# Five column blocks for six in the first MLP layer, and a shorter activation, in a windowed-attention and two-MLP kernel

## The chip, the cores and the metric

The kernel runs on one core of one Trainium2 chip. The metric is the device time of one execution in microseconds; times before are from three runs on the chip, and one further execution was profiled.

## The reference

Inputs are q, k, v of 4 batches, 8 heads, 576 positions and 64 dimensions in float32, and two pairs of weights in float64: w_in (512 x 2048) and w_out (2048 x 512), one pair for each MLP.

```
scores = (1/8) q @ k^T
heads 0-3: keep 0 <= i-j < 32;  heads 4-7: keep 0 <= i-j < 128 and (i-j) % 4 == 0
attn = softmax(scores) @ v                     # then laid out as x: 2304 tokens x 512
h = x @ w_in;  x = (h * 1/(1+exp(-1.702 h))) @ w_out      # first MLP
h = x @ w_in2; out = (max(h, 0)^2) @ w_out2               # second MLP
```

## The kernel before, in words

**Layout.** Activations lie transposed: the 512 features are four groups of 128 partitions, the tokens are columns. In the first layer the 2304 columns are cut in six blocks (`BLOCKS1`) of 512, 256, 384, 512, 256 and 384 columns. A block is a list of pieces (batch, residue of the position modulo 4, from, to), so a block's columns come from one or two batches. The second layer has five blocks (`BLOCKS2`): 512, 256, 512, 512, 512.

**A step.** For each block sixteen steps (`step`) run over the 2048 hidden features, 128 at a time. Operands are split in a high part that the matmul's float32r format holds and a remainder, and each product is three matmuls: high x high, high x low and low x high. A step is 12 matmuls into a hidden tile h (lines 587 to 589), the activation on ScalarE and VectorE (lines 609 to 645), its rounding gh and remainder gl, and 12 matmuls from them into four output banks o (lines 673 to 675), which collect over all sixteen steps. h has two PSUM banks, o four, s (scores, transposes and values of attention) two. At a block's last step the o banks are evacuated to ost tiles (two places) and stored to x2d in DRAM; the second layer loads them from there and splits them.

**The activation of the first layer** is formed as min(exp(1.702 h), 1) x h x (1 + |tanh(0.851 h)|), twice the wanted value; the evacuation scales by 0.5. It takes tanh and the exponential on ScalarE, the absolute value on ScalarE or VectorE, and two products on VectorE (lines 626 and 629). The second layer has a relu and a square.

**Weights.** Each layer has 32 weight tiles, two a step. One is loaded as float64 bits (`raw`, three places), the top half word of each number is copied to a tile c by a cast (line 309, by the helper at line 236 or 238; c has three places), joined with the rest by VectorE (line 312), and split in wh and wl. The first layer's tiles are prepared while block 0 runs and stay for all blocks; the second layer's take their places in the last block of the first layer, each when its last reader is done.

**Attention.** A batch is eight units (a pair of heads and half of the positions). A unit loads qk and v, makes 12 scores matmuls (line 451), masked maxima on VectorE (467), exponentials on ScalarE (474), a normalisation (242 or 244), a transpose (on TensorE at line 524 and a copy for batches 0 and 1, 32 x 32 bands on VectorE into a cleared tile pt for batches 2 and 3, line 509), 12 value matmuls (543), and copies of the result, high and remainder, to the x tile of the block that owns the columns (555 and 559). Batch 0 runs ahead of the first layer, batch 1 in block 0, batch 2 in block 2 and batch 3 in block 3. The x tiles have three places x0, x1, x2 for blocks n, by n modulo 3, of 512, 256 and 384 columns.

**Order.** No order is written out. `Schedule` is a planner: each task has estimated costs on the engines that may do it, predecessors, buffers and a due time (want). It takes, again and again, the task that can start first by its own clock, ties by the due time, and so fixes each engine's instruction order; which of ScalarE and VectorE does a copy is its choice too, with penalties against VectorE (`SPARE_ACT`). Due times of block steps follow from `begin`, which adds up matmul times and an allowance for attention (`T_ATT`); those of attention units are spread over the block that holds their batch. The estimates affect the order only.

Of the kernel before, what the change touches and what calls it, by code (L numbers as in the profile page):

```python
# [35 lines left out]
UQ, UK, UV = HALF, HALF + PAD, NBLK * P  # L36

T_START = 26.0
T_ATT = 12.0
A0 = 0.0  # L40
A1 = 1.0
DEFER = 0.0
BAND_FROM = 2
W2_GAP = 4.0
WARM = 256
MASK_AT = -9.0
LEAD = (12.0, 8.0, 5.0)
SPACE = 4.0
C_BUFS = 3
RAW_BUFS = 3  # L50
IDLE = (0.3, 0.3)
SPARE_POOL = (3.0, 3.0, 0.0)
# [1 line left out]
SPARE_TO = (15.0, 160.0)  # L54


_HALF_BLOCKS = [
# [3 lines left out]
]  # L61
BLOCKS1 = [[(b + g, r, a, e) for b, r, a, e in blk] for g in (0, 2) for blk in _HALF_BLOCKS]
BLOCKS2 = [512, 256, 512, 512, 512]


class Schedule:
# [18 lines left out]
    def buffer(self, cls):  # L85
        return {"cls": cls, "held": False, "left": 0, "end": 0.0}

    def task(self, engine, cost, want, fn, after=(), bufs=(), port=False):


        many = isinstance(engine, tuple)
        t = {
            "ways": dict(zip(engine, cost)) if many else {engine: cost}, "many": many,
            "want": want, "fn": fn, "bufs": bufs, "port": port,
            "left": 0, "ready": [], "next": [], "n": len(self.tasks), "end": None,
        }
        for a in after:
            a["next"].append(t)
            t["left"] += 1
        for b in bufs:  # L100
            b["left"] += 1
        self.tasks.append(t)
        return t
# [83 lines left out]
def attention_mlp_mlp(  # L187
# [33 lines left out]

    places = {
        "o": 4, "h": 2, "s": 2, "raw": RAW_BUFS, "c": C_BUFS, "qk": 2, "v": 3, "sm": 2, "st": 3, "pt": 1,
        "x0": 1, "x1": 1, "x2": 1, "xx": 1, "raw2": 3, "g": 2, "e": 1, "gh": 2, "gl": 2, "ost": 2,
    }
    for f in range(KF):
        for part in range(2):
# [37 lines left out]
    def dve1(n):  # L265
        return 0.062 + n / 960
# [20 lines left out]
    def weights(layer, f, part, want):  # L287


        m = {}  # L290
        raw_b, c_b, w_b = buffer("raw"), buffer("c"), buffer(f"w{f}_{part}")
        name = f"{f}_{part}"

        def load():

            m["raw"] = wst.tile([P, DM, 2], U32, tag="raw", bufs=RAW_BUFS, name="raw")
            nc.sync.dma_start(
                m["raw"].rearrange("p n t -> p (n t)").bitcast(U16)[:, 0:4 * DM - 1],
                (w1, w2)[layer][f, part].bitcast(U16)[:, 1:4 * DM],
            )  # L300

        def top(e):

            m["c"] = tops[top_count[0] % C_BUFS]
            top_count[0] += 1
            halves = m["raw"].rearrange("p n t -> p (n t)").bitcast(BF16).rearrange("p (n t) -> p n t", t=4)[:, :, 2]
            copy(e, m["c"].bitcast(F16).rearrange("p (n t) -> p n t", t=2)[:, :, 1], halves)

        def join():
            V.scalar_tensor_tensor(
                out=m["raw"][:, :, 0], in0=m["raw"][:, :, 0], scalar=13, in1=m["c"],
                op0=ALU.logical_shift_right, op1=ALU.bitwise_or,
            )

        def value():
            return m["raw"][:, :, 0].bitcast(F32)

        def high_part(e):  # L320
            wh[layer, f, part] = wpool.tile([P, DM], F32R, tag="wh" + name, name="wh" + name)
            copy(e, wh[layer, f, part], value())

        def low_part(e):
            wl[layer, f, part] = wpool.tile([P, DM], F32R, tag="wl" + name, name="wl" + name)
            minus(e, wl[layer, f, part], value(), wh[layer, f, part])

        t = task("dma", 1.456, want - LEAD[0], load, (), [raw_b])
        t = task(("act", "dve"), (0.57, 0.602), want - LEAD[1], top, [t] + tops_zero, [raw_b, c_b], True)
        t = task("dve", 0.602, want - LEAD[1], join, [t], [raw_b, c_b], True)  # L330
        hi = task(*copies(DM), want - LEAD[2], high_part, [t], [raw_b, w_b], True)
        lo = task(*pairs(DM), want - LEAD[2], low_part, [hi], [raw_b, w_b], True)
        split_task[layer, f, part] = [hi, lo]
        wbuf[layer, f, part] = w_b


    x_t, x_buf, x_done = {}, {}, {}
    x_first = {}

    def x_tile(n):  # L340
        if n not in x_t:
            size = 512 if n % 3 == 0 else sum(e - a for _, _, a, e in BLOCKS1[n])
            x_t[n] = xpool.tile([P, 2, KD, size], F32R, tag=f"x{n % 3}", name=f"x{n % 3}")
        return x_t[n]

    def x_pieces(b, p, u):
# [57 lines left out]
    def attend(b, p, u, want, start, turn_pe, i):  # L404
# [144 lines left out]
        att_tasks.append(pv)  # L549
        for n, w, src_, dst_ in x_pieces(b, p, u):  # L550
            if n not in x_buf:
                x_buf[n] = buffer(f"x{n % 3}")

            def to_hi(e, n=n, src_=src_, dst_=dst_):
                copy(e, dst_(x_tile(n), 0), src_(m["o"]))

            def to_lo(n=n, src_=src_, dst_=dst_):
                x = x_tile(n)
                V.tensor_tensor(out=dst_(x, 1), in0=src_(m["o"]), in1=dst_(x, 0), op=ALU.subtract)  # L559

            t = task(("act", "dve"), (0.07 + w / 1340, dve1(w)), want, to_hi, [pv], [pv_b, x_buf[n]])
            t2 = task("dve", dve1(w), want, to_lo, [t], [pv_b, x_buf[n]])
            x_done.setdefault((n, p), []).extend([t, t2])
# [5 lines left out]
    def step(layer, blk, f, want, a=0, z=None):  # L569
# [29 lines left out]
        def g():  # L599
            if "g" not in m:  # L600
                m["g"] = gpool.tile([P, 512], F32, tag="g", name="g")[:, 0:n]
            return m["g"]

        def h():
            return m["h"][:, 0:n]

        if layer == 0:

            e_b = buffer("e")

            def tanh():
                A.activation(out=g(), in_=h(), func=AF.Tanh, scale=0.851)  # L612

            def exp():
                m["e"] = gpool.tile([P, 512], F32, tag="e", bufs=1, name="e")[:, 0:n]
                A.activation(out=m["e"], in_=h(), func=AF.Exp, scale=1.702)

            def absolute(e):
                if e == "act":
                    A.activation(out=g(), in_=g(), func=AF.Abs)  # L620
                else:
                    gb = g().bitcast(U32)
                    V.tensor_scalar(out=gb, in0=gb, scalar1=0x7FFFFFFF, scalar2=None, op0=ALU.bitwise_and)

            def times_h():
                V.scalar_tensor_tensor(out=g(), in0=g(), scalar=1.0, in1=h(), op0=ALU.add, op1=ALU.mult)  # L626

            def times_e():
                V.scalar_tensor_tensor(out=g(), in0=m["e"], scalar=1.0, in1=g(), op0=ALU.min, op1=ALU.mult)  # L629

            a1 = task("act", 0.145 + n / 1536, want, tanh, [t], [h_b, g_b])
            a2 = task("act", 0.145 + n / 1536, want, exp, [t], [h_b, e_b])
            a1 = task(*copies(n), want, absolute, [a1], [g_b], True)
            a1 = task("dve", dve1(n), want, times_h, [a1], [g_b, h_b])
            last = task("dve", dve1(n), want, times_e, [a1, a2], [g_b, e_b], True)
        else:

            def relu():
                A.activation(out=g(), in_=h(), func=AF.Relu)  # L639

            def square(e):
                by_name[e].tensor_tensor(out=g(), in0=g(), in1=g(), op=ALU.mult)  # L642

            t = task("act", 0.145 + n / 1536, want, relu, [t], [h_b, g_b])
            last = task(*pairs(n), want, square, [t], [g_b], True)
# [96 lines left out]

    begin = []
    now = T_START
    att_blocks = (0, 2, 3)
    for n, size in enumerate(sizes1):
        begin.append(now)
        now += KF * 24 * mm(size) + (T_ATT if n in att_blocks else 0)
    begin2 = []
    for size in BLOCKS2:  # L750
        begin2.append(now)
# [4 lines left out]
        attend(0, p, u, T_START - (nu - i) * SPACE, True, True, i)  # L756
    if WARM:
        task("pe", 0.0, T_START, warm_end, list(att_tasks), [warm_b])
    for b in range(1, B):
        if b == BAND_FROM:  # L760
            zero_task = task(
                "pool", 0.7, begin[att_blocks[b - 1]] - 5, lambda: G.memset(pt, 0.0), list(att_tasks), [buffer("pt")]
            )
        blk = att_blocks[b - 1]
        span = begin[blk + 1] - begin[blk]
        for i, (p, u) in enumerate(ORDER):
            late = span * DEFER if b % 2 and i >= nu - 2 else 0.0
            attend(b, p, u, begin[blk] + span * (A0 + A1 * i / nu) + late, False, b < BAND_FROM, b * nu + i)

    def order(layer):  # L770
        ks = [(f, 0) for f in range(2)]
# [34 lines left out]
    for n, size in enumerate(BLOCKS2):  # L806
        c0 = sum(BLOCKS2[:n])
        want = begin2[n]
        cls = ("xx", "x1", "x0", "xx", "x0")[n]
        blk = {"i": n, "n": size, "c0": c0, "buf": buffer(cls), "done": {}}  # L810
        blk["x"] = lambda blk=blk: blk["tile"]
        blk["ready"] = lambda k, blk=blk: blk["done"][k]
# [122 lines left out]
```

## Time and profile before

| what | value |
|---|---|
| runs | 902.05, 902.67, 903.28 us (median 902.67) |
| profiled execution | 902.65 us |
| span of its instructions | 900.5 us |
| mean granted clock | 0.997 of 2.4 GHz |
| ScalarE, VectorE busy | 447.5, 506.0 us |
| HBM read, written | 54.73, 9.44 MB |

The span runs from the first to the last instruction of the core; the execution's time has 2.15 us around it. Busy times are sums over the whole span, over stages that differ, so a share of the span says little about one stage. A matmul's recorded duration overlaps its neighbours': what a stream of them costs is read from start to start.

### The profile page before, as it was taken

What the parts mean: (1) busy time and instruction counts of PE and PEld (TensorE: products, weight loads), DVE (VectorE), ACT (ScalarE), POOL (GpSimd) and SP (SyncE); (2) the same over time, 40 slices, a digit from 0 to 9 for tenths busy, and PEclk for the clock granted to TensorE, in tenths of its full rate; (3) what the DMA queues carried; (4) which work ended last, traced back from release to release, by engine and by line L of the source; (5) the groups of instructions that cost most, each with busy time, mean ns of one, the idle gap of its engine ahead of it and who ended that gap; (6) DMA issues with size and microseconds to landing.
All of it is one profiled execution on the core that took longest, in us unless ns stands there. A gap on an engine that the chain in (4) does not pass through costs nothing.

```text
span 900.5 us, 13900 instructions
## 1 busy us (share of the span) xinstructions
PE 884.7 (98%) x5145; PEld 758.4 (84%) x5145; DVE 506.0 (56%) x1427; ACT 447.5 (50%) x1211; POOL 2.6 (0%) x10
## 2 busy tenths in 40 slices
PE   7899999999999999999999999999999999999998
PEld 5677778999998777899999788899888888888887
DVE  6888887646788777755989722242322332222223
ACT  7999998545557555543666622232322222222222
POOL 0000000000000000000000000000000000000000
PEclk9999999999999999999999999999999999999999
DMA  6555563101122110110755500020000010000001
GB/s 227 187 156 195 194 208 133 32 12 44 47 58 83 34 44 16 54 60 1 247 194 194 189 1 0 1 94 1 24 1 0 13 48 1 1 23 24 1 1 47
DMA packets 28115, 65.06 MB, mean 72 GB/s; under 512 B 3120, under 2 KB 10800, under 8 KB 28048
## 3 DMA queue, kind: packets, MB, share of 16 engines
q1 hardware_dynamic: 28048, 64.18, 21.8%
q8 instruction: 40, 0.66, 0.3%
q14 instruction: 27, 0.22, 0.1%
HBM read 54.73 MB, written 9.44 MB: 71 GB/s over the span
## 4 chain that ended last, share of the span: by engine, by line
PE 74%; ACT 11%; DVE 7%; DMA 6%; issue 2%; SPq 0%; DVEq 0%; ACTq 0%
PE h L587 12%; PE o L673 12%; PE h L588 12%; PE h L589 12%; PE o L675 12%; PE o L674 12%; DMA raw<-in_w 5%; ACT sm L474 2%; ACT c L236 2%; ACT sm L242 2%; PE s L451 2%; DVE wl L247 1%; PE pv L543 1%; DVE g L626 1%; DVE g L629 1%
## 5 line engine op out<-in xcount | busy, mean ns | idle before, releaser
L673 PE MATMUL o<-gh,wh 128*128 128x512 f32 (+2 forms) x704 | 248.6, 353 | 1.9 <-ACT ost L242 1.2
L675 PE MATMUL o<-gl,wh 128*128 128x512 f32 (+2 forms) x704 | 247.6, 352 | 0.4 <-DVE gl L247 0.3
L674 PE MATMUL o<-gh,wl 128*128 128x512 f32 (+2 forms) x704 | 246.4, 350 | 0.0
L587 PE MATMUL h<-x,wh 128*128 128x512 f32 (+2 forms) x580 | 203.2, 350 | 1.2 <-DVE g L626 1.0
L589 PE MATMUL h<-x,wl 128*128 128x512 f32 (+2 forms) x580 | 198.8, 343 | 0.5 <-DVE wl L247 0.5
L588 PE MATMUL h<-x,wh 128*128 128x512 f32 (+2 forms) x580 | 198.6, 342 | 0.0
L642 DVE TENSOR_TENSOR g<-g 128x512 f32<-128x512 f32 (+1 forms) x81 | 51.2, 632 | 205.3 <-ACT g L639 204.6
L639 ACT ACTIVATE g<-h 128x512 f32<-128x512 f32 (+1 forms) x81 | 44.5, 550 | 219.0 <-PE h L589 218.0
L673 PEld LDWEIGHTS o<-gh,wh 128*128 128x128 f32 x704 | 132.9, 189 | 20.1 <-ACT gh L236 1.9
L675 PEld LDWEIGHTS o<-gl,wh 128*128 128x128 f32 x704 | 132.8, 189 | 18.8 <-DVE gl L247 3.2
L236 ACT CAST gh<-g 128x512 fp32r<-128x512 f32 (+2 forms) x166 | 90.2, 543 | 112.9 <-DVE g L629 55.7
L674 PEld LDWEIGHTS o<-gh,wl 128*128 128x128 f32 x704 | 132.9, 189 | 14.7
L247 DVE TENSOR_TENSOR gl<-g,gh 128x512 fp32r<-128x512 f32 (+2 forms) x177 | 104.4, 590 | 67.2 <-ACT gh L236 64.1
L587 PEld LDWEIGHTS h<-x,wh 128*128 128x128 f32 x580 | 110.3, 190 | 15.5 <-DVE g L626 1.7
L589 PEld LDWEIGHTS h<-x,wl 128*128 128x128 f32 x580 | 110.0, 190 | 11.0 <-DVE wl L247 0.8
L588 PEld LDWEIGHTS h<-x,wh 128*128 128x128 f32 x580 | 110.2, 190 | 9.9 <-DVE x L559 0.8
L474 ACT ACTIVATE sm<-sm,st 96x128 f32<-96x128 f32 x180 | 70.6, 395 | 12.7 <-DVE st L467 12.7
L612 ACT ACTIVATE g<-h 128x512 f32<-128x512 f32 (+2 forms) x96 | 46.8, 488 | 52.1 <-PE h L589 50.7
L626 DVE SCALAR_TENSOR_TENSOR g<-g,h 128x512 f32<-128x512 f32 (+2 forms) x96 | 52.7, 550 | 16.9 <-ACT g L620 13.0
L629 DVE SCALAR_TENSOR_TENSOR g<-e,g 128x512 f32<-128x512 f32 (+2 forms) x96 | 53.1, 553 | 1.2
L589 PE MATMUL h<-xx,wl 128*128 128x512 f32 x128 | 49.8, 389 | 0.0
L588 PE MATMUL h<-xx,wh 128*128 128x512 f32 x128 | 49.8, 389 | 0.0
(70 smaller groups left out, 831.0 us busy)
## 6 DMA issues: line engine op xcount, KB each, us to landing
raw<-in_w SPq DMA_DIRECT2D x64, 511.8 KB, 4.0
qk<-in_qkv SPq DMA_DIRECT2D x32, 304.0 KB, 2.9
v<-in_qkv SPq DMA_DIRECT2D x32, 192.0 KB, 2.9
raw<-x2d SPq DMA_DIRECT2D x16, 256.0 KB, 2.9
out_T<-ost SPq DMA_DIRECT2D x14, 256.0 KB, 2.1
x2d<-ost SPq DMA_DIRECT2D x8, 256.0 KB, 2.3
x2d<-ost SPq DMA_DIRECT2D x8, 192.0 KB, 2.0
x2d<-ost SPq DMA_DIRECT2D x8, 128.0 KB, 2.6
```

What stands on the lines that cost most here:

```text
L236: A.copy(out, in_)
L247: by_name[e].tensor_tensor(out=out, in0=a, in1=b, op=ALU.subtract)
L474: A.activation(out=m["sm", j][:, i], in_=m["sm", j][:, i], func=AF.Exp, bias=m["st"][:, 0, j, i:i + 1], scale=-1.0, accum_out=m["st"][:, 1 ...
L587: T.matmul(out, w_hi[:, ks], x[:, 0, k, a:z], start=(k == 0), stop=False)
L588: T.matmul(out, w_hi[:, ks], x[:, 1, k, a:z], start=False, stop=False)
L589: T.matmul(out, w_lo[:, ks], x[:, 0, k, a:z], start=False, stop=(k == KD - 1))
L626: V.scalar_tensor_tensor(out=g(), in0=g(), scalar=1.0, in1=h(), op0=ALU.add, op1=ALU.mult)
L629: V.scalar_tensor_tensor(out=g(), in0=m["e"], scalar=1.0, in1=g(), op0=ALU.min, op1=ALU.mult)
L642: by_name[e].tensor_tensor(out=g(), in0=g(), in1=g(), op=ALU.mult)
L673: T.matmul(out, w_hi[:, ds_], m["gh"], start=(f == 0 or extra), stop=False)
L674: T.matmul(out, w_lo[:, ds_], m["gh"], start=False, stop=False)
L675: T.matmul(out, w_hi[:, ds_], m["gl"], start=False, stop=(f == KF - 1))
```

## The change

The first layer has five blocks of 512, 512, 256, 512 and 512 columns; the second layer's blocks become 512, 512, 256, 512, 512. Places of x are assigned by a list: blocks 0 and 3 have x0 (512), 1 and 4 have x2 (512), 2 has x1 (256). Batch 1's eight units stay in block 0, batch 2's go to block 1, six of batch 3's to block 2 and two to block 3 (`UNITS`); the allowance is 2.4 us a unit in place of 12 us a batch. The activation is h x (1 + tanh(0.851 h)), with no exponential, absolute value or second product, and the tile e is gone. The c tiles are two for three. The estimate of the cast to c becomes 0.67 us on ScalarE and 0.38 us on VectorE, from 0.57 and 0.602. `DEFER`, which was 0, is gone, and pt is cleared with a due time of 8 us ahead of batch 2's first unit, from 5 us ahead of its block.

```diff
-T_ATT = 12.0
+T_ATT = 2.4
-C_BUFS = 3
+C_BUFS = 2
-_HALF_BLOCKS = [
+BLOCKS1 = [
     [(0, 0, 0, 144), (0, 1, 0, 144), (0, 2, 0, 144), (0, 3, 0, 80)],
-    [(0, 3, 80, 144), (1, 0, 0, 144), (1, 1, 0, 48)],
-    [(1, 1, 48, 144), (1, 2, 0, 144), (1, 3, 0, 144)],
+    [(0, 3, 80, 144), (1, 0, 0, 144), (1, 1, 0, 144), (1, 2, 0, 144), (1, 3, 0, 16)],
+    [(1, 3, 16, 144), (2, 0, 0, 128)],
+    [(2, 0, 128, 144), (2, 1, 0, 144), (2, 2, 0, 144), (2, 3, 0, 144), (3, 0, 0, 64)],
+    [(3, 0, 64, 144), (3, 1, 0, 144), (3, 2, 0, 144), (3, 3, 0, 144)],
 ]
-BLOCKS1 = [[(b + g, r, a, e) for b, r, a, e in blk] for g in (0, 2) for blk in _HALF_BLOCKS]
-BLOCKS2 = [512, 256, 512, 512, 512]
+UNITS = (8, 8, 6, 2)
+BLOCKS2 = [512, 512, 256, 512, 512]
...
-        t = task(("act", "dve"), (0.57, 0.602), want - LEAD[1], top, [t] + tops_zero, [raw_b, c_b], True)
+        t = task(("act", "dve"), (0.67, 0.38), want - LEAD[1], top, [t] + tops_zero, [raw_b, c_b], True)
...
+    x_place = ("x0", "x2", "x1", "x0", "x2")
...
-            e_b = buffer("e")
             def tanh():
                 A.activation(out=g(), in_=h(), func=AF.Tanh, scale=0.851)
-            def exp():
...
-            def absolute(e):
...
             def times_h():
                 V.scalar_tensor_tensor(out=g(), in0=g(), scalar=1.0, in1=h(), op0=ALU.add, op1=ALU.mult)
-            def times_e():
-                V.scalar_tensor_tensor(out=g(), in0=m["e"], scalar=1.0, in1=g(), op0=ALU.min, op1=ALU.mult)
             a1 = task("act", 0.145 + n / 1536, want, tanh, [t], [h_b, g_b])
-            a2 = task("act", 0.145 + n / 1536, want, exp, [t], [h_b, e_b])
-            a1 = task(*copies(n), want, absolute, [a1], [g_b], True)
-            a1 = task("dve", dve1(n), want, times_h, [a1], [g_b, h_b])
-            last = task("dve", dve1(n), want, times_e, [a1, a2], [g_b, e_b], True)
+            last = task("dve", dve1(n), want, times_h, [a1], [g_b, h_b])
...
-    att_blocks = (0, 2, 3)
-        now += KF * 24 * mm(size) + (T_ATT if n in att_blocks else 0)
+        now += KF * 24 * mm(size) + (T_ATT * UNITS[n] if n < len(UNITS) else 0)
...
+    wants = []
+    for n, count in enumerate(UNITS):
+        span = begin[n + 1] - begin[n]
+        wants += [begin[n] + span * A1 * (A0 + i) / count for i in range(count)]
...
-            attend(b, p, u, begin[blk] + span * (A0 + A1 * i / nu) + late, False, b < BAND_FROM, b * nu + i)
+            attend(b, p, u, wants[(b - 1) * nu + i], False, b < BAND_FROM, b * nu + i)
...
-        cls = ("xx", "x1", "x0", "xx", "x0")[n]
+        cls = ("xx", "x0", "x1", "x2", "xx")[n]
```

## Rows read from the trace of the kernel before

**Rows 1.** The page: engine, busy us (share of the span), instructions.

```profile
PE 884.7 (98%) x5145; PEld 758.4 (84%) x5145; DVE 506.0 (56%) x1427; ACT 447.5 (50%) x1211; POOL 2.6 (0%) x10
```

**Rows 2.** Four stretches: length, busy (instructions) by engine, granted clock, DMA share, GB/s.

```profile
19.00:47.00 28.00, 24.68 (x218) 17.14 (x215) 25.57 (x139) 27.95 (x122) 0.00 (x0) 1.00 0.55 175
47.00:147.00 100.00, 98.98 (x570) 77.91 (x570) 83.82 (x222) 96.08 (x266) 0.58 (x1) 0.98 0.57 188
...
275.40:378.20 102.80, 102.80 (x587) 81.33 (x586) 79.70 (x283) 59.61 (x188) 0.00 (x0) 1.00 0.15 46
...
427.90:500.90 73.00, 72.06 (x399) 67.63 (x398) 65.39 (x130) 50.21 (x100) 0.00 (x0) 1.00 0.66 215
```

**Rows 3.** TensorE in order of time, two second-layer blocks: start us, duration us, what.

```profile
639.72 0.39 PE L589 MATMUL h<-x,wl 128*128 128x512 f32 x1
...
644.93 0.39 PE L674 MATMUL o<-gh,wl 128*128 128x512 f32 x1
...
599.79 0.28 PE L675 MATMUL o<-gl,wh 128*128 128x256 f32 x1
...
602.91 0.28 PE L588 MATMUL h<-x,wh 128*128 128x256 f32 x1
```

**Rows 4.** Groups by line, TensorE, 47 to 147 us: count | busy us, mean ns.

```profile
L543 PE MATMUL pv<-pt,v 128*64 128x96 f32 x96 | 6.5, 256 | 0.5 <-ACT pt L236 0.5
L451 PE MATMUL s<-qk 64*96 64x128 f32 x84 | 6.3, 282 | 0.0
L524 PE MATMUL tp<-ident,sm 96*128 96x96 f32 x42 | 5.6, 253 | 0.0
```

**Rows 5.** Groups by line, TensorE, 275.4 to 378.2 us.

```profile
L451 PE MATMUL s<-qk 64*96 64x128 f32 x86 | 6.8, 282 | 0.0
L543 PE MATMUL pv<-pt,v 128*64 128x96 f32 x108 | 6.4, 254 | 0.0
```

**Rows 6.** Chain that ended last, attention in blocks 2 and 3: start us, us, what.

```profile
213.33 0.83 PE s L451 x12
...
274.60 0.83 PE s L451 x12
...
348.08 0.65 PE pv L543 x12
...
360.90 0.65 PE pv L543 x12
```

**Rows 7.** Waits, 47 to 147 us: who for whom, us in total, times, longest.

```profile
DVE raw L312 <- ACT c L236: 4.2, 11, 0.6
...
PE h L587 <- DVE g L626: 1.0, 1, 1.0
```

**Rows 8.** One stretch, columns as in rows 2.

```profile
49.40:52.80 3.40, 3.40 (x10) 2.62 (x9) 3.27 (x8) 3.29 (x10) 0.00 (x0) 0.50 0.50 182
```

**Rows 9.** Waits, 427.9 to 510 us.

```profile
PEld o L675 <- DVE gl L247: 2.6, 8, 0.6
PEld o L673 <- ACT gh L236: 1.9, 4, 0.6
...
PE o L673 <- ACT ost L242: 1.2, 1, 1.2
```

**Rows 10.** Groups by line and shape, whole span: count | busy us, mean ns | idle before.

```profile
L236 ACT CAST c<-raw 128x512 f16<-128x512 bf16 x53 | 40.3, 782 | 10.9 <-DMA raw<-in_w 10.7
...
L629 DVE SCALAR_TENSOR_TENSOR g<-e,g 128x512 f32<-128x512 f32 x32 | 21.9, 684 | 0.1
...
L616 ACT ACTIVATE e<-h 128x512 f32<-128x512 f32 x32 | 19.0, 595 | 0.1
...
L629 DVE SCALAR_TENSOR_TENSOR g<-e,g 128x384 f32<-128x384 f32 x32 | 17.7, 552 | 0.2
...
L620 ACT ACTIVATE g<-g 128x512 f32<-128x512 f32 x16 | 10.2, 637 | 0.0
...
L238 DVE CAST c<-raw 128x512 f16<-128x512 bf16 x11 | 5.1, 462 | 3.9 <-DMA raw<-in_w 3.8
```

More of the change, by code (lines that the diff above doesn't have):

```diff
@@ L38 @@
 T_START = 26.0
-T_ATT = 12.0
+T_ATT = 2.4
 A0 = 0.0
 A1 = 1.0
-DEFER = 0.0
 BAND_FROM = 2
@@ L223, in attention_mlp_mlp @@
         "o": 4, "h": 2, "s": 2, "raw": RAW_BUFS, "c": C_BUFS, "qk": 2, "v": 3, "sm": 2, "st": 3, "pt": 1,
-        "x0": 1, "x1": 1, "x2": 1, "xx": 1, "raw2": 3, "g": 2, "e": 1, "gh": 2, "gl": 2, "ost": 2,
+        "x0": 1, "x1": 1, "x2": 1, "xx": 1, "raw2": 3, "g": 2, "gh": 2, "gl": 2, "ost": 2,
     }
@@ L341, in x_tile @@
         if n not in x_t:
-            size = 512 if n % 3 == 0 else sum(e - a for _, _, a, e in BLOCKS1[n])
-            x_t[n] = xpool.tile([P, 2, KD, size], F32R, tag=f"x{n % 3}", name=f"x{n % 3}")
+            size = sum(e - a for _, _, a, e in BLOCKS1[n])
+            x_t[n] = xpool.tile([P, 2, KD, size], F32R, tag=x_place[n], name=x_place[n])
         return x_t[n]
@@ L551, in attend @@
             if n not in x_buf:
-                x_buf[n] = buffer(f"x{n % 3}")
+                x_buf[n] = buffer(x_place[n])
             def to_hi(e, n=n, src_=src_, dst_=dst_):
@@ L607, in step @@
         if layer == 0:
-            e_b = buffer("e")
             def tanh():
                 A.activation(out=g(), in_=h(), func=AF.Tanh, scale=0.851)
-            def exp():
-                m["e"] = gpool.tile([P, 512], F32, tag="e", bufs=1, name="e")[:, 0:n]
-                A.activation(out=m["e"], in_=h(), func=AF.Exp, scale=1.702)
-            def absolute(e):
[L619 to L623, printed above, removed]
             def times_h():
                 V.scalar_tensor_tensor(out=g(), in0=g(), scalar=1.0, in1=h(), op0=ALU.add, op1=ALU.mult)
-            def times_e():
-                V.scalar_tensor_tensor(out=g(), in0=m["e"], scalar=1.0, in1=g(), op0=ALU.min, op1=ALU.mult)
             a1 = task("act", 0.145 + n / 1536, want, tanh, [t], [h_b, g_b])
-            a2 = task("act", 0.145 + n / 1536, want, exp, [t], [h_b, e_b])
-            a1 = task(*copies(n), want, absolute, [a1], [g_b], True)
-            a1 = task("dve", dve1(n), want, times_h, [a1], [g_b, h_b])
-            last = task("dve", dve1(n), want, times_e, [a1, a2], [g_b, e_b], True)
+            last = task("dve", dve1(n), want, times_h, [a1], [g_b, h_b])
         else:
@@ L758, in attention_mlp_mlp @@
         task("pe", 0.0, T_START, warm_end, list(att_tasks), [warm_b])
+    wants = []
+    for n, count in enumerate(UNITS):
+        span = begin[n + 1] - begin[n]
+        wants += [begin[n] + span * A1 * (A0 + i) / count for i in range(count)]
     for b in range(1, B):
         if b == BAND_FROM:
[L761 to L765, printed above, removed]
+            zero_task = task("pool", 0.7, wants[(b - 1) * nu] - 8, lambda: G.memset(pt, 0.0), list(att_tasks), [buffer("pt")])
         for i, (p, u) in enumerate(ORDER):
-            late = span * DEFER if b % 2 and i >= nu - 2 else 0.0
-            attend(b, p, u, begin[blk] + span * (A0 + A1 * i / nu) + late, False, b < BAND_FROM, b * nu + i)
+            attend(b, p, u, wants[(b - 1) * nu + i], False, b < BAND_FROM, b * nu + i)
     def order(layer):
```

## The prediction

> **What bounds the kernel now.** I read the page's busy line first: TensorE holds 98% of the span [rows 1]. Such a share says neither how many columns are streamed nor what stands between matmuls, so the second view is the table by stretch, cut where the width of the blocks changes [rows 2]. There the reader is to see three regimes. From 19 to 47 us ScalarE has no gap (27.95 of 28 us): it works off the first batch's attention. From 47 to 147 us, block 0, ScalarE is busy 96 of 100 us and VectorE 84, while TensorE is nearly full. In 427.9 to 500.9 us, the last block of the first layer, VectorE is busy 65.4 of 73 us. Elsewhere TensorE alone is full.
>
> Third, the price of a matmul, from start to start. Two starts of the 512-wide stretch are 23 matmuls apart: 5.21 / 23 = 226.5 ns; two of the 256-wide one 26 apart: 3.12 / 26 = 120.0 ns [rows 3]. A line through both has 0.416 ns a column and 13.5 ns whatever the width; it gives 173.3 ns at 384. These two are the ruler for what follows.
>
> In block 0's 100 us from 47 us on TensorE issues 570 matmuls [rows 2], 222 of them attention's [rows 4]. So 348 belong to the layer, 12 of these (the next block's first step) 256 wide: 336 x 0.2265 + 12 x 0.12 = 77.5 us. In the stretch 275.4 to 378.2 us the same count gives 587 - 194 = 393 [rows 2, 5]: 360 at 512, 24 at 384, 9 at 256, together 86.8 us. In the chain twelve scores matmuls take 0.83 us and twelve of the value product 0.65 [rows 6], so 69 and 54 ns each: the later stretch's attention is 86 x 69 + 108 x 54 = 11.8 us, and 102.8 - 86.8 - 11.8 = 4.2 us is lost in the switches of about eight units, 0.5 us a unit. I count that half microsecond as part of a unit. Block 0's attention is 84 x 69 + 96 x 54 = 11.0 us, and its 42 transposes about 2.9 us (an estimate, at a scores matmul's price). 100 - 77.5 - 13.9 = 8.6 us; less 8 x 0.5 for switches, 4.6 us are lost. The waits name 1.0 us of it: the third hidden step waits for the line-626 product to free an h bank [rows 7]. From 49.4 to 52.8 us the granted clock is 0.50, the 1.2 GHz level, which after a start with TensorE waiting costs half of 3.4, 1.7 us [rows 8]. The other 1.9 us are small.
>
> The last block has 399 matmuls in 73.0 us [rows 2]; its few 512- and 256-wide ones balance about 384, so 399 x 0.1733 = 69.1 and 3.9 us are lost. The waits there are weight loads for the projection held up by gl and gh [rows 9]: the activation's chain comes late behind the second layer's weights. Right behind it stands 1.2 us for the evacuation of an o bank.
>
> **The change, part by part.** *Blocks.* The columns stay 2304. A block has 16 steps of 24 matmuls, so six blocks issue 2304 matmuls and five 1920. 384 x 13.5 ns = 5.2 us less, all on the path, since TensorE is the full engine in every stretch. The second layer has the same four 512 blocks and one 256, in another order: nothing. Four x2d stores fewer, of larger pieces, lie beside matmuls. A rule speaks against this term. The row has 13.5 ns a matmul [rows 3]; the Trainium skill ("TensorE: Matmul & The Clock Gate", section "Back-to-back issue gap") puts the spacing at the streaming time plus about 2.5 ns, by which, an estimate from that page, 384 matmuls would be 1.0 us. The measured spacing decides.
>
> *Last block, 512 for 384 columns.* Its steps grow from 24 x 0.1733 = 4.16 to 24 x 0.2265 = 5.44 us, with the same two weights a step to load and split. VectorE loses sixteen line-629 products of 552 ns (8.8 us) and some absolute values; its product and its remainder of each step grow by 0.13 us, 32 of them, 4 us [rows 10]. So some 60 us of work stand in 16 x 5.44 = 87 us instead of 65 in 73. The waits on gl and gh should go: -3.5 us of 3.9. Bounds: none returns (0), all of it and the 1.2 us of the o bank (-5.1). That o bank's evacuation comes at the change of layers, where the weights are loaded after as before, so I let it stay.
>
> *Activation.* Before, the chain is tanh, exponential, absolute value, two products, rounding and remainder; after, tanh, one product, rounding, remainder. In block 0 that takes from ScalarE 16 x 0.595 = 9.5 us of exponentials and up to 10.2 us of absolute values, and from VectorE 16 x 0.684 = 10.9 us [rows 10]. Of the 96 and 84 busy us about 76 and 73 are left. But the path is TensorE's, and only its 4.6 lost us can come back. The wait on line 626 should go: tanh and product no longer stand on either side of two ScalarE instructions. I take that 1.0 and half of the small 1.9: -2.0 us. Bounds: 0 (ScalarE's hidden time only turns into idling) and -4.6 (the clock stays up too). In the blocks without weights to split, the removed work lies beside matmuls: 0.
>
> *Estimate.* The copy of the weights' top halves is priced 0.67 and 0.38 us for 0.57 and 0.602; the rows have 0.782 on ScalarE and 0.462 on VectorE [rows 10], so the plan moves some to VectorE. From 19 to 47 us ScalarE has no gap [rows 2], and VectorE's 25.6 of 28 us leave little room. I take 0; as ends, two copies fewer or more on the path, -1.5 and +1.5.
>
> *Units moved.* Batch 1 stays in block 0. Batch 2 goes into a 512 block, six units of batch 3 into the 256 block and two behind it. Their 16 units, of scores, value product and switch, cost TensorE the same. Their loads go with them, on queues that are idle for most of those stretches (DMA share 0.15) [rows 2]. Behind a late unit in TensorE's queue stands the next block's hidden step, which needs its columns. A clear of pt moves with batch 2; GpSimd has nothing else to do. I take 0; ends 0 and +3 (the 256 block's last unit late).
>
> *Places.* Two c tiles for three: a tile is held for a cast and a join, 0.78 us and one about as long as the 684 ns product [rows 10], 1.5 us, so two serve a weight every 0.75 us where about 3 us are needed. The join waits for the cast in block 0, not the cast for a place [rows 7]. Cost 0; at most +1. The x places are freed a block or more ahead of their next writer; 0.
>
> The sum: 5.2 + 3.5 + 2.0 = 10.7 us less. The profiled execution took 902.65 us, 2.15 more than its span; the median of the runs is 902.67, so it stands for them. 902.65 - 10.7 = 892.0 us.
>
> **Rivals.** *A, only the count pays.* TensorE is already 98% busy [rows 1], ScalarE's relief falls into time that matmuls cover, and the last block's lost time turns into other waits (o banks, DMA). 902.65 - 5.2 = 897.5. For it: the list of TensorE's own waits is short. Against: the 3.9 us have a named cause that the change eases twice. *B, more comes back.* Block 0 is freed of all 4.6, the clock stays up, the o bank's 1.2 goes and start-up gives 1: 5.2 + 3.9 + 1.2 + 4.6 + 1.0 = 15.9, 886.8. For it: the whole second half of the list hangs on the engines that are relieved. *C, slower: the 256 block is paced by attention.* It lasts 384 x 0.12 = 46.1 us plus six units of 0.83 + 0.65 + 0.5: 58 us, 9.7 a unit. Seven scores from 213.3 to 274.6 us are 10.2 us apart, in the 512 block value products 12.8 [rows 6]. If a unit's chain through both engines can't go faster than 12.8 us, six take 76.8 and TensorE stands still for 18.7: 902.65 - 10.7 + 18.7 = 910.7. It turns the sign from 11.5 us a unit. Against it: 12.8 is no more than that block's 102.8 us over its eight units, 10.2 near the same for the 384 block, so the pace looks like the plan's, not a limit. *D, the 13.5 ns are no price of a matmul* but come with something that stays (the stream itself at its end). Then the count gives nothing and 902.65 - 5.5 = 897.2 is left. Against: start to start is what TensorE needs for one, and nothing else shows in it. By the page of the Trainium skill named above the time would be 902.65 - 5.5 - 1.0 = 896.2, an estimate.
>
> **How the numbers follow.** Forecast 0.58, A 0.20, B 0.13, C 0.05, D 0.04. 892.0 us is the forecast's. The range runs from about all fast ends together (5.2 + 5.1 + 4.6 + 1.5 = 16.4, so 886.3, put at 886.5) to A (897.5); it holds A's, B's and D's times, half of A's spread, and leaves out C and the edges. Faster than by 0.2% (1.8 us, what a measurement can tell from none): the forecast, A, B and D with a little off for mishaps, 0.92; C 0.05 slower; 0.03 the same.
>
> **What would show it.** After: some 384 fewer TensorE instructions at the same spacing; the last block's 399-odd matmuls with under 0.5 us beyond their spacing, and no waits on gl or gh; no wait for line 626 near 49 us; ScalarE in block 0 under 90% busy; the 1.2 us at the change of layers still there. I am wrong where the 256 block lasts over 60 us, where TensorE waits for an x copy at a block's start, or where the first full hidden step begins later than 44 us.

## The result, and the profile after

The changed kernel takes 891.79 us (median of 4 runs, 889.98 to 892.49) for 902.36: a ratio of 0.9882, 95% interval 0.9865 to 0.9899. The forecast was 892.0 us in 886.5 to 897.5. The execution profiled after is the quickest of the four, 889.98 us with a span of 888.0; a second profiled execution of it (f0_same below) took 892.37, nearer the median.

The page's busy line of the changed kernel, beside [rows 1]:

```profile
PE 873.6 (98%) x4761; PEld 719.9 (81%) x4761; DVE 436.2 (49%) x1231; ACT 388.3 (44%) x1035; POOL 2.1 (0%) x9
```

TensorE has 5145 - 4761 = 384 instructions fewer and the same 98%. The spacing is the one of [rows 3]: two starts 23 matmuls apart in the second layer, 5.22 / 23 = 227 ns.

```profile
559.65 0.39 PE L592 MATMUL h<-xx,wl 128*128 128x512 f32 x1
...
564.87 0.39 PE L658 MATMUL o<-gh,wl 128*128 128x512 f32 x1
```

The same table by stretch as [rows 2] (columns there): start, block 0, the 256 block with six attention units, the last block of the first layer.

```profile
17.40:45.00 27.60, 24.95 (x213) 17.13 (x214) 22.85 (x133) 27.45 (x120) 0.00 (x0) 1.00 0.51 156
45.00:147.40 102.40, 101.41 (x575) 78.61 (x575) 76.58 (x203) 87.06 (x242) 0.58 (x1) 1.00 0.57 190
252.80:309.70 56.90, 56.52 (x518) 52.97 (x517) 44.45 (x199) 31.41 (x126) 0.00 (x0) 1.00 0.20 63
398.90:489.00 90.10, 89.05 (x388) 72.22 (x387) 68.17 (x120) 48.40 (x78) 0.00 (x0) 1.00 0.58 194
```

ScalarE is at 85% in block 0 (96% before; the prediction's sum had about 76) and still without a gap at the start. The 256 block lasts 56.9 us. The last block has 387 matmuls (the view counts one more at its edge): 387 x 0.2267 = 87.7 us, so 2.4 us are lost.

That subtraction, made for every stage from the starts of TensorE's instructions, is the ledger below: the time up to a stage's last projection, less the matmuls issued by then, at 226.7, 173.3 or 120 ns by width and 69, 54 and 83 ns for attention's scores, values and transposes. What is left is lost time in us.

| kernel | start, to the second hidden step's end | first two projections | rest of block 0 | attention blocks | last block, first layer | change of layers | rest | sum |
|---|---|---|---|---|---|---|---|---|
| before | 22.6 | 4.3 | 5.0 | 8.8 | 4.4 | 1.6 | 0.1 | 46.7 |
| after | 21.5 | 1.7 | 4.9 | 7.7 | 2.4 | 0.8 | 0.0 | 38.9 |
| f0_same (after again) | 22.2 | 1.7 | 6.4 | 7.7 | 2.2 | 1.2 | 0.0 | 41.3 |
| e2_new_act | 22.5 | 1.4 | 6.9 | 7.1 | 5.0 | 0.9 | 1.0 | 44.8 |
| e3_old_est | 22.5 | 2.2 | 7.5 | 7.2 | 2.2 | 0.0 | 0.0 | 41.6 |
| e4_split_l2 | 22.1 | 1.6 | 5.4 | 7.7 | 3.5 | 0.9 | 0.5 | 41.7 |
| e5_old_act_b0 | 23.4 | 4.0 | 6.8 | 9.3 | 2.3 | 0.4 | 0.0 | 46.2 |
| e6_old_act_b4 | 22.9 | 1.6 | 5.4 | 7.7 | 1.9 | 1.0 | 0.0 | 40.6 |
| e7_dma_est | 28.3 | 1.2 | 3.8 | 7.2 | 0.0 | 0.0 | 0.0 | 40.5 |
| e8_dma_spare | 28.3 | 1.0 | 3.6 | 7.5 | 0.0 | 0.0 | 0.5 | 40.9 |
| e9_before_dma | 26.2 | 1.6 | 6.0 | 11.0 | 0.7 | 0.2 | 0.0 | 45.5 |
| f1_l2_loads | 23.1 | 1.6 | 5.7 | 7.7 | 0.0 | 0.0 | 0.0 | 38.2 |
| f2_spareto | 24.1 | 0.5 | 4.8 | 7.5 | 0.0 | 0.0 | 0.1 | 37.0 |
| f3_late_loads | 22.2 | 1.7 | 5.2 | 7.8 | 0.0 | 0.0 | 0.0 | 36.9 |

The matmuls' own sum falls from 793.9 to 788.8 us, 5.1. The lost time falls by 7.8 in the first profile after and by 5.4 in the second; start and block 0 alone differ by 2.2 between these two executions of one program (0.7 and 1.5), the last block by 0.2. So a single profile tells the loss of start and block 0 to about 1.5 us, and smaller differences there are not told from chance below.

The waits of [rows 7], block 0 of the changed kernel, and of [rows 9], its last block to 500 us:

```profile
DVE raw L314 <- ACT c L238: 7.6, 11, 1.8
...
PE h L590 <- ACT wh L238: 0.8, 1, 0.8
```

```profile
ACT c L238 <- DMA raw<-in_w: 19.5, 15, 2.9
...
PEld o L659 <- DVE gl L249: 1.8, 3, 0.8
...
PEld o L657 <- ACT gh L238: 1.2, 2, 0.7
```

TensorE's hidden step in block 0 no longer waits for the product (line 626 before, 616 now) but 0.8 us for a weight's high part. In the last block the waits on gl and gh have become fewer, not none. And [rows 8] has its counterpart at full clock:

```profile
49.40:52.80 3.40, 3.40 (x16) 2.77 (x15) 2.09 (x6) 3.40 (x15) 0.00 (x0) 1.00 0.33 110
```

### The profile page after: what moved, and what is told of

Same layout as the page of the kernel before. It is cut to its first block, busy times and chain, and to the rows that moved or that the text cites. A ratio compares the mean times of both kernels' runs of the same rounds, so it can differ in the third digit from the quotient of the medians.

```text
span 888.0 us, 12713 instructions
## 1 busy us (share of the span) xinstructions
PE 873.6 (98%) x4761; PEld 719.9 (81%) x4761; DVE 436.2 (49%) x1231; ACT 388.3 (44%) x1035; POOL 2.1 (0%) x9
## 4 chain that ended last, share of the span: by engine, by line
PE 85%; DVE 5%; DMA 4%; ACT 4%; issue 1%; SPq 0%; DVEq 0%; ACTq 0%
PE o L657 14%; PE h L590 14%; PE o L659 14%; PE o L658 13%; PE h L592 13%; PE h L591 13%; DMA raw<-in_w 3%; PE s L454 2%; PE pv L546 2%; DVE wl L249 1%; ACT sm L477 1%; ACT sm L244 1%; DVE raw L314 1%; PE tp L527 1%; ACT c L238 1%
## 5 line engine op out<-in xcount | busy, mean ns | idle before, releaser
L657 PE MATMUL o<-gh,wh 128*128 128x512 f32 (+1 forms) x640 | 237.3, 371 | 0.3 <-ACT gh L238 0.3
L659 PE MATMUL o<-gl,wh 128*128 128x512 f32 (+1 forms) x640 | 235.7, 368 | 0.6 <-DVE gl L249 0.4
L658 PE MATMUL o<-gh,wl 128*128 128x512 f32 (+1 forms) x640 | 235.1, 367 | 0.0
L590 PE MATMUL h<-x,wh 128*128 128x512 f32 (+1 forms) x512 | 190.9, 373 | 1.9 <-DVE g L616 0.8
L592 PE MATMUL h<-x,wl 128*128 128x512 f32 (+1 forms) x512 | 186.2, 364 | 0.5 <-DVE wl L249 0.5
L591 PE MATMUL h<-x,wh 128*128 128x512 f32 (+1 forms) x512 | 186.0, 363 | 0.1
L623 ACT ACTIVATE g<-h 128x512 f32<-128x512 f32 (+1 forms) x81 | 44.5, 550 | 222.9 <-PE h L592 222.8
L659 PEld LDWEIGHTS o<-gl,wh 128*128 128x128 f32 x640 | 120.6, 188 | 22.6 <-DVE gl L249 2.6
L249 DVE TENSOR_TENSOR gl<-g,gh 128x512 fp32r<-128x512 f32 (+1 forms) x161 | 101.7, 634 | 64.8 <-ACT gh L238 62.2
L238 ACT CAST gh<-g 128x512 fp32r<-128x512 f32 (+1 forms) x149 | 85.9, 580 | 87.3 <-DVE g L626 54.4
L613 ACT ACTIVATE g<-h 128x512 f32<-128x512 f32 (+1 forms) x80 | 43.9, 552 | 77.6 <-PE h L592 75.8
L616 DVE SCALAR_TENSOR_TENSOR g<-g,h 128x512 f32<-128x512 f32 (+1 forms) x80 | 50.2, 629 | 54.1 <-ACT g L613 53.4
L314 DVE SCALAR_TENSOR_TENSOR raw<-raw,c 128x512 uint32<-128x512 uint32 x64 | 44.1, 691 | 21.3 <-ACT c L238 21.0
L470 DVE CUSTOM_DVE_ANT_0 sm<-s,mask_sb 96x128 f32<-96x128 f32 x180 | 41.6, 281 | 24.8 <-PE s L454 23.7
```

Source lines behind the costliest of these rows:

```text
L238: A.copy(out, in_)
L249: by_name[e].tensor_tensor(out=out, in0=a, in1=b, op=ALU.subtract)
L314: V.scalar_tensor_tensor(out=m["raw"][:, :, 0], in0=m["raw"][:, :, 0], scalar=13, in1=m["c"], op0=ALU.logical_shift_right, op1=ALU.bitwise_or,
L590: T.matmul(out, w_hi[:, ks], x[:, 0, k, a:z], start=(k == 0), stop=False)
L591: T.matmul(out, w_hi[:, ks], x[:, 1, k, a:z], start=False, stop=False)
L592: T.matmul(out, w_lo[:, ks], x[:, 0, k, a:z], start=False, stop=(k == KD - 1))
```

## The experiments

e2, e4, e5 and e6 ran on one chip, e3, e7, e8 and e9 on a second and f0 to f3 on a third; the kernel before took 902.42, 901.34 and 901.23 us there, and each ratio is to that time of the same chip.

**The activation alone: e2_new_act.** The kernel before, with the short activation.

```diff
-            a2 = task("act", 0.145 + n / 1536, want, exp, [t], [h_b, e_b])
-            a1 = task(*copies(n), want, absolute, [a1], [g_b], True)
-            a1 = task("dve", dve1(n), want, times_h, [a1], [g_b, h_b])
-            last = task("dve", dve1(n), want, times_e, [a1, a2], [g_b, e_b], True)
+            last = task("dve", dve1(n), want, times_h, [a1], [g_b, h_b])
```

> The kernel before with the short activation alone (six blocks, three c tiles, old estimate). Theory: no matmul is saved, so 5.1 us of the gain are missing; what TensorE lost comes back where the long chain caused it: about 2.6 us in the first steps of block 0 (the h wait and the half clock behind it) and about 2 of the 4.4 us lost in the last block. 902.4 - 4.6 = 897 to 898 us, with 5145 TensorE instructions as before. Rival A (relief on ScalarE and VectorE falls into covered time): no gain, 902 us.

Measured: 899.5 us, ratio 0.9967 (0.9956 to 0.9979). Of some 4.6 us of gain expected, 2.9 came. The first two projections gain 2.9 us, where about 2.6 was expected, and there is no half clock near 50 us. The last block gains nothing: it loses 5.0 us for 4.4, although VectorE is busy 55.4 of 72 us there, for 65.4 of 73 before. So neither a shorter chain nor less load on VectorE gave that block anything. The rest of block 0 lost 1.9 us more, little beyond what two executions of one program differ by there.

```profile
425.00:497.00 72.00, 69.50 (x393) 66.50 (x392) 55.38 (x104) 43.59 (x77) 0.00 (x0) 1.00 0.66 217
```

**What a matmul costs whatever its width: e4_split_l2.**

```diff
-BLOCKS2 = [512, 512, 256, 512, 512]
+BLOCKS2 = [512, 512, 256, 256, 256, 512]
-        cls = ("xx", "x0", "x1", "x2", "xx")[n]
+        cls = ("xx", "x0", "x1", "x2", "x1", "xx")[n]
```

> The changed kernel with one 512 block of the second layer cut in two of 256 columns: 384 matmuls more, no column more, in a stage where TensorE loses nothing. Theory: 384 x 13.3 ns = +5.1 us, so 896.9 us. Rival D (the fixed part is no price of a matmul): 0, 891.8 us. By the 2.5 ns a matmul of the Trainium skill (TensorE: Matmul & The Clock Gate, Back-to-back issue gap): +1.0, 892.8 us, an estimate.

Measured: 898.84 us, ratio 0.9963 (0.9950 to 0.9976); 7.0 us above f0_same by the medians, on two chips, and 4.9 between the two profiled executions, of which e4's is its quickest. The total is thus a rough price; part of its excess is in stages that the edit was not aimed at (the first layer's last block loses 3.5 us for 2.2). The stage itself is read from two stretches of its profile, a 512 block and the two 256 blocks that cover as many columns:

```profile
578.60:665.30 86.70, 86.70 (x385) 71.86 (x384) 22.89 (x33) 21.29 (x35) 0.00 (x0) 1.00 0.03 13
665.40:758.30 92.90, 92.90 (x773) 92.56 (x772) 32.60 (x77) 29.98 (x75) 0.00 (x0) 1.00 0.09 29
```

In the first 383 matmuls start (three of them narrow), 226.4 ns each; in the second 771, 120.5 ns each, with the 0.4 us in them that the ledger's column "rest" has for the added change of blocks. At the ledger's 226.7 and 120.0 ns, 768 narrow ones take 5.1 us more than 384 wide ones. Rival D falls: here the fixed part is 13.3 ns a matmul. The 1.0 us worked out from the Trainium skill ("TensorE: Matmul & The Clock Gate", "Back-to-back issue gap") falls with it.

**The long activation in one block: e5_old_act_b0 and e6_old_act_b4.** Both are the changed kernel with the old tasks in block 0 or in the last block alone (the edit is shown in part).

```diff
+            if blk["i"] == 0:          # e6: len(BLOCKS1) - 1
+                e_b = buffer("e")
...
-WARM = 256
+WARM = 192
-"raw2": 3
+"raw2": 2
```

> The changed kernel with the long activation in block 0 alone (to make place for its tile, the warm-up matmuls are 192 columns for 256 and the second layer's load tiles two for three). Theory: the short chain saved the wait of the third hidden step and the half clock behind it: 1.0 to 3.9 us come back, 893 to 895.5 us, nearly all before the second projection, little in the rest of block 0. Rival (start-up went better for another reason, the corrected estimate or the changed due times): no difference from the changed kernel, 891.8 us, and no wait of a hidden step on the product.

> The changed kernel with the long activation in the first layer's last block alone (same two small changes as the run before). Theory (width and chain both eased the last block): of the 2.0 us that the last block lost less, about half comes back, 892.5 to 893.5 us, with more waits on gh and gl. Rival 1 (width alone did it, 5.44 us a step leave room for any chain): 891.8 us. Rival 2 (the chain alone did it): +2 or more, 894 us.

Measured: e5 897.44 us, ratio 0.9948 (0.9931 to 0.9965); e6 891.28 us, ratio 0.9878 (0.9865 to 0.9892). In e5 the half clock is back, and the first two projections lose 4.0 us for 1.6 in e6. TensorE's waits from 46 to 60 us, and the stretch behind:

```profile
PE s L454 <- DVE x L562: 1.7, 1, 1.7
```

```profile
50.40:53.80 3.40, 3.40 (x11) 2.53 (x9) 3.34 (x6) 2.82 (x7) 0.00 (x0) 0.50 0.53 155
```

The wait is not the one that the theory named. No hidden step waits for the product; attention's scores wait 1.7 us for a copy to x, which frees their bank. In ScalarE's order the tanh, the exponential and the absolute value of a step, 46.83 to 48.44 us, stand ahead of that copy. So the long activation brings a TensorE wait and the half clock back, but through another operation that stands behind it in ScalarE's order.

The whole price, 6.2 us beside e6 by the medians, is more than the theory's 3.9: the rest of block 0 has 1.4 of it (within the spread there) and the attention blocks behind 1.6. In the last block the long chain costs nothing (1.9 us lost, 2.2 without it), as rival 1 of e6 has it: in steps of 512 columns the chain's length makes no difference.

**The estimate: e3_old_est.**

```diff
-        t = task(("act", "dve"), (0.67, 0.38), want - LEAD[1], top, [t] + tops_zero, [raw_b, c_b], True)
+        t = task(("act", "dve"), (0.57, 0.602), want - LEAD[1], top, [t] + tops_zero, [raw_b, c_b], True)
```

> The changed kernel with the old estimate of the cast to c (0.57 and 0.602 us). Theory (the corrected estimate gave the 0.5 to 1.1 us that start-up became shorter, and lets block 0 plan ScalarE rightly): 1 to 2.5 us slower than the changed kernel, 893 to 894 us, the first full hidden step again about 45.5 us after the start. Rival (the start-up differs from run to run by that much, the estimate does nothing): 891.5 us.

Measured: 891.51 us, ratio 0.9884 (0.9866 to 0.9902). The rival holds: no difference from the changed kernel.

**What the last block still loses: e7_dma_est, e8_dma_spare, e9_before_dma.** e7 and e9 let the plan think every transfer 1.41 times as long, in the changed kernel and in the one before; e8 is e7 with a smaller penalty.

```diff
-                moved = max(issued + 0.65, moved) + cost
+                moved = max(issued + 0.65, moved) + 1.41 * cost
-SPARE_ACT = (0.0, 1.0, 0.0)
+SPARE_ACT = (0.0, 0.3, 0.0)        # e8 alone
```

> The changed kernel with the planner's estimate of a transfer 1.41 times as long (two weight tiles issued 0.6 us apart land 2.06 us apart in the changed kernel's last block, and the plan has 1.456). Theory (the last block's remaining 2.4 us come from casts that stand in ScalarE's queue waiting for a load that lands later than planned, with gh behind them): the last block loses under 1.2 us, 890.0 to 890.8 us in all. Rival 1 (the three raw places set the pace, whatever the plan thinks): the last block still loses 2 us or more, 891.5 us. Rival 2 (VectorE's load makes gl late): the same, with no casts waiting ahead of gh.

> The kernel before with the same longer transfer estimate. Theory (in its last block a weight is needed every 2.1 us and three raw places can't turn over that fast, so a wait in the queue stays wherever it is put): the last block still loses 3 to 4.4 us, 901.5 to 902.5 us. Rival (wrong order alone was the cause there too): it loses under 2 us, 899.5 us.

> As e7_dma_est, and the plan's penalty against VectorE for copies that either engine may do is 0.3 us for 1.0 in the first layer's block 0. Theory (block 0 is held by single chains, no longer by ScalarE's load): within 0.7 us of e7_dma_est. Rival (ScalarE's queue still paces block 0, whose later part loses 4.9 us as before): 1.5 to 3 us faster than e7_dma_est.

Measured: e7 891.1 us (ratio 0.9880, 0.9863 to 0.9897), e8 892.24 (0.9897, 0.9880 to 0.9914), e9 900.41 (0.9992, 0.9980 to 1.0005). In e7 the last block loses nothing, but the start loses 6 us more, so the total, expected under 890.8 us, hides it. Why the start suffers is not settled. In e9 the last block loses 0.7 us for 4.4: my theory, that three raw places could not turn over fast enough, falls. Part came back in the block ahead (2.4 us for 0.0), and its total can't be told from no change. e8 shows no gain from freeing ScalarE further, so its rival falls; it is 1.1 us above e7, outside the theory's 0.7, but with overlapping intervals.

**The estimate of the second layer's loads alone: f0_same, f1_l2_loads; and two more: f2_spareto, f3_late_loads.**

```diff
-        t = task("dma", 1.456, want - LEAD[0], load, (), [raw_b])
+        t = task("dma", (1.456, 2.06)[layer], want - LEAD[0], load, (), [raw_b])                # f1, f2
+        t = task("dma", 2.06 if layer or f > 2 else 1.456, want - LEAD[0], load, (), [raw_b])   # f3
-SPARE_TO = (15.0, 160.0)
+SPARE_TO = (30.0, 160.0)     # f2
```

> The changed kernel again, unaltered, for its own spread beside the next three: 891.5 us, start-up up to the first full hidden step losing 21.5 to 22.5 us, the last block 2.4 to 3.5 us; no stretch at the 1.2 GHz level near 50 us. If the half clock comes back here, its absence was chance and not the short chain.

> The changed kernel with the longer estimate (2.06 us) for the second layer's weight tiles alone. Theory (casts that wait in the queue for a late load, with gh and gl behind them, are what the last block still loses): start-up and block 0 as in the changed kernel, the last block under 0.3 us, 2 to 3.5 us faster than f0_same, 888.5 to 889.5 us. Rival (the last block was smooth in e7_dma_est because start-up had delayed everything ahead of it): no difference, 891.5 us.

> As f1_l2_loads, and the penalty against VectorE begins at due times of 30 us for 15, so that the last units of batch 0 may use VectorE freely. Theory (ScalarE without a gap sets the start): the first full hidden step 1 to 2 us earlier, 887.5 us. Rival (VectorE is as full there): same as f1_l2_loads or slower by up to 1 us.

> As f1_l2_loads, and the longer estimate for the first layer's tiles from the fourth step on as well, so that the start keeps the short one. Theory (casts that wait for late loads cost block 0 the 1.5 us too by which it lost less in e7_dma_est): 1 to 1.5 us faster than f1_l2_loads. Rival (that gain belonged to the later start, which had let weights run ahead): same as f1_l2_loads.

Measured: f0 891.84 us (0.9889, 0.9869 to 0.9910), f1 888.96 (0.9855, 0.9834 to 0.9876), f2 887.60 (0.9848, 0.9821 to 0.9874), f3 888.07 (0.9849, 0.9829 to 0.9869). f1 is 2.9 us below f0 by the medians, as expected. The ledger has 2.2 us gone in the last block, where they were looked for, and 1.2 more at the change of layers behind it. Both last blocks, f0 then f1:

```profile
401.10:491.10 90.00, 88.76 (x389) 72.27 (x388) 66.94 (x118) 47.47 (x77) 0.00 (x0) 1.00 0.57 193
```

```profile
401.40:489.10 87.70, 87.70 (x388) 72.63 (x387) 65.69 (x112) 52.77 (x85) 0.00 (x0) 1.00 0.58 198
```

TensorE's work is the same. ScalarE has 5.3 us more to do in f1 and VectorE 1.3 us less, so ScalarE was not relieved; what changed is the order, and the engine of a few copies. In order of time (start us, duration us, engine, what; in brackets the idle time before it and what ended it) f0 has:

```profile
468.30 0.78 ACT L238 CAST c<-raw 128x512 f16<-128x512 bf16 x1 [3.06 <-DMA raw<-in_w]
...
469.12 0.69 DVE L314 SCALAR_TENSOR_TENSOR raw<-raw,c 128x512 uint32<-128x512 uint32 x1 [1.70 <-ACT c L238]
...
469.40 0.39 PE L592 MATMUL h<-x,wl 128*128 128x512 f32 x1
...
469.90 0.65 ACT L238 CAST wh<-raw 128x512 fp32r<-128x512 f32 x1 [0.81 <-DVE raw L314]
...
471.10 0.78 ACT L238 CAST c<-raw 128x512 f16<-128x512 bf16 x1 [0.55 <-DMA raw<-in_w]
...
471.75 0.58 ACT L613 ACTIVATE g<-h 128x512 f32<-128x512 f32 x1
...
472.53 0.68 DVE L616 SCALAR_TENSOR_TENSOR g<-g,h 128x512 f32<-128x512 f32 x1
...
473.26 0.50 PE L590 MATMUL h<-x,wh 128*128 128x512 f32 x1 [0.75 <-DVE g L616]
```

The step's last hidden matmul runs from 469.40 to 469.79 us, and its tanh begins at 471.75, 2.0 us later. Ahead of it in ScalarE's order stand a rounding that waits for a join, which waited for a cast, which had waited 3.06 us for a load, and a second cast that waits for the next load. So the product frees the h bank late and TensorE waits 0.75 us. TensorE's wait names the product, as those of [rows 9] name gl and gh; the cause stands three places further back. In f1 a cast waits for a load as well, but each tanh follows soon on the matmul that it needs:

```profile
467.71 0.78 ACT L238 CAST c<-raw 128x512 f16<-128x512 bf16 x1 [1.34 <-DMA raw<-in_w]
468.94 0.60 ACT L613 ACTIVATE g<-h 128x512 f32<-128x512 f32 x1 [0.45 <-PE h L592]
469.78 0.67 ACT L238 CAST wh<-raw 128x512 fp32r<-128x512 f32 x1 [0.24 <-DVE raw L314]
470.35 0.78 ACT L238 CAST c<-raw 128x512 f16<-128x512 bf16 x1
471.66 0.60 ACT L613 ACTIVATE g<-h 128x512 f32<-128x512 f32 x1 [0.53 <-PE h L592]
```

The same holds for the whole block. From the recorded end of a step's last hidden matmul to its tanh, the sixteen steps take 0.37 us on average and 1.97 at most in f0, 0.10 and 0.37 in f1; in the kernel before 1.07 and 2.90, in e2 0.60 and 1.30, in e9 0.23 and 0.70.

The estimate that helps is not the truer one. The planner lets a load alone land 0.45 + 0.65 + 1.456 + 0.9 = 3.46 us after issue; in f0's last block the 29 loads take 3.71 us on average, one issued alone about 3.2. The 12 that take over 3.6, up to 5.0, were each issued while another transfer was under way. With 2.06 a lone load has 4.06 us in the plan. So f1 plans with slack for the late ones. Beside the planner's own times, f0's tanh is 4.7 us late in the first step of that block and 7.0 in its last, f1's 5.0 and 4.8: in f0 the plan falls behind by as much as the block loses, in f1 it does not.

f2 and f3 are lower still by 1.4 and 0.9 us, which their intervals don't tell from f1; f2's first full hidden steps are not earlier (24.1 us lost at the start), so its theory did not come true where it looked, and f3's 1 to 1.5 us are not shown. Any of the three beats both kernels; f2 and f3 are 1.5% under the kernel before.

## Why the prediction was right, and where not

The forecast of 892.0 us met the measured 891.79, and the largest term, the count, is shown by itself (e4). That the total came within 0.2 us is luck in part, as the terms show, against f0_same, whose profiled time is 10.3 us below that of [rows 1]'s execution:

| term | predicted | measured |
|---|---|---|
| 384 matmuls fewer | -5.2 | -5.1 |
| last block of the first layer | -3.5 | -2.2 (first profile -2.0) |
| block 0 | -2.0 | -2.6 in the first two projections, +1.4 in the rest (first profile -2.6 and -0.1) |
| start | 0 | -0.4 (first profile -1.1) |
| attention blocks | 0 | -1.1 |
| change of layers | 0 | -0.4 |

The last block, block 0 and the count together gave 2.2 us less than forecast, and the terms set at 0 gave 1.9 more. These made up for one another.

*The count* holds to a tenth, and e4's second layer prices it by itself: TensorE had no other loss there, so each matmul's fixed part is on the path.

*The last block* came out smaller, and its cause was wrong. (Its loss before was a little larger than the sum's 3.9 us: the view's 399 holds three matmuls that only overlap the window's edges, and the ledger has 4.4.) The step that failed is "the activation's chain comes late behind the second layer's weights", eased "twice", by width and by the shorter chain, with VectorE's load as the measure. A shorter chain gave nothing there (e2, e6), and less load on VectorE nothing either (e2). What held TensorE were casts of the weights that wait for a load, put ahead of the activation in the engines' order by a plan without slack for late loads: with a longer estimate the loss goes (e7, e9, f1). That the wider steps let the first half of it go is argued by elimination (e3, e6); no run has the wide blocks alone. The other half needed the estimate.

*Block 0* is right in size by the first profile (-2.7) and short by the second (-1.2), where the rest of block 0 varies by 1.5. That the long activation costs the half clock and some 2.4 us in the first two projections is shown (e5), by another wait than the product's. The half clock's part had been taken as a bound only and not in the sum. That the rest of block 0 gives back half of its small losses is not borne out. What the chain is worth depends on the rest of the kernel: 2.9 us in the old blocks (e2), 5.6 to 6.2 in the new ones (e5 beside f0 and e6). Why the attention blocks take part in that was not settled.

*The estimate* was rightly taken as 0, for a wrong reason: the plan moved no cast to VectorE. ScalarE made 53 of 64 before [rows 10] and makes 54:

```profile
L238 ACT CAST c<-raw 128x512 f16<-128x512 bf16 x54 | 42.0, 781 | 27.3 <-DMA raw<-in_w 23.7 <-DVE gl L249 2.1 <-DVE wh L240 1.3
```

*Units moved, places*: nothing was lost; the attention blocks gained 1.1 us. The moved units, the places of x and the two c tiles were not tested one by one. The 256 block's six units cost 2.7 us of lost time, under half a microsecond each, and rival C fell: the scores come in pairs there, and from 259.91 to 278.01 us two units take 18.1 us, 9.1 each, below the 11.5 at which the sign would have turned. So the 12.8 of [rows 6] was no limit of a unit's chain.

```profile
259.91 0.83 PE s L454 x12
264.17 0.83 PE s L454 x12
...
278.01 0.83 PE s L454 x12
282.26 0.83 PE s L454 x12
```

*The signs*: the count, the spacing, line 626, ScalarE under 90% and the 256 block under 60 us came as said. The last block's "under 0.5 us" and "no waits on gl or gh" did not, and the 1.2 us of the o bank, said to stay, is gone: from 489 to 580 us TensorE waits only 0.3 us, for gh.

Rival A's reason, that relief on the other engines would be covered, held in the later part of block 0 and, for the activation, in the last block; B's 886.8 us was approached only by f1 to f3, with another edit.

## What to carry to other kernels

Where one engine is full in every stage, price the change by counting its instructions and their fixed part; here that term came out to a tenth, the waits around it did not. A wait that TensorE names can be several places from its cause: look in the feeding engine's queue for an operation that waits for a load ahead of the one that is needed. Where a plan fixes the order, compare its times with the trace, transfers too, and leave slack where they vary: here one number for 32 loads was worth 2.9 us, over a quarter of the whole change's 10.6, and the same factor for all transfers only moved the loss to the start.

## What the runs showed of the hardware

Two weight tiles of 512 KB issued 0.6 us apart in the changed kernel's last block landed 3.2 and 4.6 us after issue, 2.06 us apart; one alone takes 3.2 us. A granted clock of 0.50, the 1.2 GHz level, stood near 50 us in both kernels with the long activation in block 0 and the old transfer estimate (from 49.4 us in the one before, from 50.4 in e5) and in none with the short one. TensorE had waited ahead of it: 0.5 us for a copy to pt and 1.0 for the product in the one before, 1.7 for a copy to x in e5. In f2 it waits 1.1 us for the product and 0.4 for a copy to x there, and the clock stays at 1.00, so the length of these waits alone does not decide it. With the longer estimate for all transfers, and its later start, it stood at 21.5 us in e9 (after waits of 1.2 and 2.2 us), at 16.1 in e8 and at 15.7 and 36.2 in e7.
